# Odd heads' k by DMA, a norm with its sums from the addition, and a staged order of the work, in a four-layer attention and FFN kernel

## The chip, the cores and the metric

The kernel runs on one core of a Trainium2 chip. The metric is the device time of one execution in microseconds (us), the median of the runs shown. TensorE is called PE in the profile, VectorE DVE, ScalarE ACT, GpSimd POOL and SyncE SP. SP issues nearly all DMAs.

## The reference

Four layers follow one another on x, which has 2048 rows of 512 bf16 numbers: attention, FFN, attention, FFN, each on the normalized x and added to it, with the same weights in both pairs.

```python
def _A_ref(x, wq, wk, wv, wo, beta):        # 32 heads of 16, 4 segments of 512 rows
    q, k, v = x @ wq, x @ wk, x @ wv        # split in heads and segments
    phi = lambda t: jnp.where(t > 0, t + 1.0, jnp.exp(t))
    M = z = 0
    for s in range(4):
        p = softmax(qs @ ks.T * Dh ** -0.5 + causal_mask)      # inside the segment
        a_mem = (phi(qs) @ M) / (phi(qs) @ z + 1e-06)          # the segments before it
        outs.append(g * a_mem + (1.0 - g) * (p @ vs))          # g = sigmoid(beta), by head
        M, z = M + phi(ks).T @ vs, z + phi(ks).sum(rows)
    return concat(outs) @ wo

def _B_ref(x, w_gate, w_up, w_down):        # inner width 1792
    return gelu(x @ w_gate) * (x @ w_up) @ w_down

x = x + _A_ref(_layernorm(x), ...); x = x + _B_ref(_layernorm(x), ...)   # and both once more
```

## The kernel before

The work is cut into eight segments of 512 rows, `k` = 0 to 7: segments 0 to 3 are the first attention and FFN, 4 to 7 the second pair on the same rows. A segment is four tiles of 128 rows. x stays in `x_sb` on the chip; all weights are loaded once.

One segment's attention: a norm writes normalized rows `xn`, which are turned into `xnT` (by DMA transposes on SP, for some norms by PE transposes with `ident`); q and k come out transposed (`q`, `kf`: four blocks `b` of 128 rows, eight heads of 16 rows each), v in rows (`vaug`). A score round is four products at once on 32-row strips of PE. Even heads take their k rows straight from `kf`. For odd heads, and for rounds that take an even and an odd head together, a copy `kx` holds k with the other heads' rows at zero: 192 columns for each 128 keys, of which the first 64 hold the even heads and the other 128 the odd ones. `masked_copies` makes it with two multiplications by a column of `masks` for each block, on DVE (L417), POOL (L417) or ACT (L422). ACT takes the exponential of each pair of rounds in two instructions (L1399), POOL or DVE masks the diagonal (L1346, L1351, L1356), and a flush (L955) multiplies by v for one block and one parity of heads; DVE divides by the sums and turns the result into `aT` (L972 to L990). `wo` products follow, and DVE adds them to x (L1028). `vz` is a copy of halves of v, by DMA (L701). phi of k is turned by DMA for the memory update (L866), phi of q feeds the memory's products.

The FFN: a norm of its own (`Norm` with key `xnTf`): once a row tile is added, DVE takes statistics (L514, L522); once all four have them, POOL adds epsilon (L527) and takes the power -1/2 (L532), DVE writes four `xn` (L544). For `k` = 0, 1 and 7 (`BY_PE`) PE turns them (L586), each behind two small dummy products (`FILL`, L584). Then come 14 gate, 14 up and 4 down products of 128 rows; ACT takes gelu, for which it loads another table.

Dense products run `whole` (L476) or as four 32-column strips at once (L471, `columns`), which follows the mode of the work around them. A change of mode takes PE some time.

The order of the instructions on every engine is written out by a planner when the kernel is built. It keeps a clock for each engine, posts jobs with a time at which they are ready and a slack, and lets PE take the item with the earliest due time, score rounds when two pairs of PSUM banks are free. `POLICY` holds the due times and slacks; `CHANGES` may replace them in windows of 20 us of the planner's time, and is empty. Where PE has nothing that is ready, the planner puts a dummy product on the tile `warm`:

```python
        if bank is not None:
            if streams:
                ps = Psum()
                ps.bank = bank
                product(ps()[:, 0:P], warm[:], wide[:, 0, :])
```

SP's queue holds DMA transposes, copies of v, weight loads and outputs in one order, and an instruction that waits holds all that are behind it.

Of the kernel before, what the change touches and what calls it, by code (L numbers as in the profile page):

```python
# [18 lines left out]
P = 128  # L19
D = 512  # L20
# [11 lines left out]
VALUES = TPS * VW + 16  # L32
SCALE = DH ** -0.5
# [11 lines left out]
PAIRED = [(ki, P * ki, C, C * ki) for ki in range(TPS)]  # L45


def round_of(t):

    b, i = divmod(t, ROUNDS)  # L50
    if i == SHARED:
        return b, (0, 1), PAIRED, None
    par = int(i > SHARED)
    return b, (par,), FULL[i - par * (SHARED + 1)], DIAG[i - par * (SHARED + 1)]


BY_PE = {("xnTf", 0), ("xnTf", 1), ("xnTf", NK - 1)}
BANKS = 8
# [3 lines left out]
URGENT, SOON, NORMAL = -4.0, -1.5, 0.0  # L62
XN_BUFS = 4
BUFS = 6
FILL = 2
# [4 lines left out]
    flush_wait=60.178, piece_slack=2.474, kb_slack=40.846, mem_slack=-55.59, margin=2.052, qk_due=-2.997, e_q=-1.628,  # L70
    e_k=2.444, exp_slack=-52.211, e_slack=213.844, phi_slack=26.757, gelu_slack=17.711, act_evict=-7.207,
    first_evict=15.014, gate_step=70.271, up_due=-0.803, up_step=0.121, down_due=2.855, down_step=15.464,
    upd_due=-0.036, kb_act=30.625, vz_slack=-37.946, x_dve=-2.928, v0_due=-11.201, x1_at=-44.439, x2_at=17.127,
    x3_at=25.097, x3_load=11.502, direct=4, gelu_tiles=7, look=4.219, lag=0.576, wv_at=-5.253, xn_pool=39.635,
    kb_pool=0.131, cut_pool=-3.745, at_pool=5.073, pe_turns=0, gate_due=2.262, shun=0.829, col_gap=3.113, hold=3,
    early=122.612, starve=0.322, near=-0.26, cap=2, soon=21.81, columns=0)

CHANGES = {
}
# [12 lines left out]
class Engine:  # L92
# [24 lines left out]
    def serve(self, now):  # L117
# [9 lines left out]
        job = min((j for j in jobs if j[0] + self.LATENCY <= start + 0.03), key=lambda j: j[0] + j[1] + (  # L127
# [123 lines left out]
class Item:  # L251


    def __init__(self, due, ready, ops, done, kind, ps, after="start"):
        self.after = after
        self.due = due if callable(due) else lambda: due
        self.ready, self.ops, self.done, self.kind, self.ps = ready, ops, done, kind, ps
        self.posted = 0.0
# [27 lines left out]
def order(pol, nc, cst, seg, wrk, psp, A_x, A_wq, A_wk, A_wv, A_wo, A_beta, B_x, B_w_gate, B_w_up, B_w_down, out):  # L286
# [88 lines left out]

    tmp_e2 = cst.tile([P, H], F32, name="tmp_e2")
# [26 lines left out]

    def on_dve_or_pool(ready, slack, later, fast, slow, emit, told):

        taken = []
        ck.dve.post(ready, slack, (fast, lambda: emit(nc.vector), told), taken=taken)
        if later is not None:
            ck.pool.post(ready, slack + later, (slow, lambda: emit(nc.gpsimd), told), taken=taken)

    def masked_copies(ready, slack, kx, kf, told):
# [4 lines left out]
        def vector(which, eng):  # L416
            return lambda: eng.tensor_scalar(out=kx[:, :, C * which:C * which + P], in0=kf, scalar1=masks[:, which:which + 1],  # L417
                                             scalar2=None, op0=ALU.mult)
# [6 lines left out]
        ck.dve.post(ready, slack, (Port(0.35), vector(0, nc.vector), None),  # L425
                    (Port(0.35), vector(1, nc.vector), told), taken=taken)
        ck.pool.post(ready, slack + pol.kb_pool, (Port(1.57, True), vector(0, nc.gpsimd), None),
# [3 lines left out]
    def turn_later(t, slack, out, in_, landed, margin=0.0):  # L431
# [5 lines left out]
        ck.sp.post(t, slack, (1.3, lambda: nc.sync.dma_start_transpose(out=out(), in_=in_()), told))  # L437
# [40 lines left out]
    def soon(name, n=KT, part=1.0):  # L478

        t = ck.pe - 0.1 - ck.back  # L480
# [20 lines left out]
    class Norm:  # L501
        def __init__(self, key, tt0, tag, slack, free):
            self.key, self.tt0, self.tag, self.slack, self.free = key, tt0, tag, slack, free
            self.mv, self.n, self.left = None, 0, TPS
# [3 lines left out]

        def stats(self, j, ready):
            def emit():  # L510
                if self.mv is None:
                    self.mv = self.small("mv", 2)
# [3 lines left out]
            def told(t):  # L516
                self.n += 1
                if self.n == TPS:
                    self.scales(t)

            ck.dve.post(ready, self.slack, (0.66, emit, None),
                        (0.17, lambda: nc.vector.bn_aggr(out=self.mv[:, j, :], in_=self.st6[:]), told))  # L522

        def scales(self, ready):
            def first():
                self.ve = wrk.tile([P, TPS, 1], F32, tag="lnve", name="ve")
                nc.gpsimd.tensor_scalar(out=self.ve[:], in0=self.mv[:, :, 1:2], scalar1=EPS_LN, scalar2=None,  # L527
                                        op0=ALU.add)

            def second():  # L530
                self.rs = self.small("rs", 1)
                nc.gpsimd.tensor_tensor(out=self.rs[:], in0=self.ve[:], in1=mhalf[:], op=ALU.pow)  # L532

            ck.pool.post(ready, URGENT, (0.25, first, None),
                         (1.05, second, lambda t: ck.when(self.free, lambda: self.start(max(t, ck.pe)))))

        def start(self, ready):
            self.xnT = seg.tile([P, KT, L], BF16, tag=self.tag, bufs=1, name="xnT")
            for j in range(TPS):
                xn_slots.take(lambda n, j=j: bufs.take(lambda i: self.row(j, n, i, max(ready, ck.pe))))  # L540

        def normed(self, j, i, eng=nc.vector):
            xn = buffer(i, "xn")
            eng.tensor_scalar(out=xn[:], in0=x_sb[:, self.tt0 + j, :], scalar1=self.mv[:, j, 0:1],  # L544
# [3 lines left out]
        def row(self, j, n, i, ready):  # L548
# [13 lines left out]
            def told(t):  # L562
                if self.by_pe():
                    items.append(self.turn_item(j, xn, t, landed))
                else:
                    turn_later(t, self.slack, lambda: self.xnT[:, :, j * P:(j + 1) * P], lambda: xn()[:], landed,
# [961 lines left out]
```

## Time and profile before

| | |
|---|---|
| runs | 541.96, 542.2 and 543.59 us, median 542.2 |
| profiled execution | 543.32 us, span 541.6 |
| granted PE clock | 1.0 |
| PE busy | 522.7 us, 97% |
| DVE busy | 439.1 us, 81% |
| ACT busy | 434.3 us, 80% |
| POOL busy | 297.4 us, 55% |
| DMA q1 | 68752 packets, 26.36 MB, 24.5% of 16 engines |

The profile is of one execution. The span runs from its first to its last instruction; its own time is 1.7 us longer. Busy times are sums over the instructions. The end of a PE product is modelled, so what PE does in a stretch is read from the starts. Behind the bar of a row stands the idle time of the engine just before it, with what ended that idle time.

### The profile page before, as it was taken

The page shows a single profiled execution, that of the slowest core. Times are in us where ns is not written, and L with a number is a line of the kernel's source. Part 1 is how long each engine was busy: PE and PEld are TensorE (multiplying, and loading weights), DVE is VectorE, ACT ScalarE, POOL GpSimd, SP SyncE. Part 2 cuts the span into 40 slices and gives each one's busy share as a digit, 9 for nine tenths or more (in the row PEclk, how much of TensorE's full clock was granted, in tenths as well). Part 3 has the DMA queues.
Part 4 walks back from the last instruction along what each step waited for, and adds up shares of the span by engine and source line. Part 5 has one row for each costly group of instructions (what it writes and reads, how often), then busy time and mean ns, then how long its engine had stood idle before and what let it go on. Part 6 is the DMA issues. An engine that isn't in the chain of part 4 may idle for free.

```text
span 541.6 us, 22747 instructions
## 1 busy us (share of the span) xinstructions
PE 522.7 (97%) x10016; PEld 274.0 (51%) x10075; DVE 439.1 (81%) x814; ACT 434.3 (80%) x533; POOL 297.4 (55%) x346
## 2 busy tenths in 40 slices
PE   8899999999999999999999999999999999999997
PEld 4454555454554445554555545554465456555444
DVE  7899998899988998679987699879778786786342
ACT  5999899997998987999899899997887978910320
POOL 4887589487857986155871595716863164300000
PEclk9999999999999999999999999999999999999999
DMA  8477410620240124101332211411313014000001
GB/s 270 63 123 178 136 41 7 153 52 14 33 79 14 24 41 89 33 2 32 42 70 32 34 34 20 72 22 33 61 33 40 15 13 81 4 3 27 14 0 40
DMA packets 69141, 28.08 MB, mean 52 GB/s; under 512 B 53426, under 2 KB 69042, under 8 KB 69042
## 3 DMA queue, kind: packets, MB, share of 16 engines
q1 hardware_dynamic: 68752, 26.36, 24.5%
q8 instruction: 79, 1.29, 1.0%
q10 hardware_dynamic: 290, 0.26, 0.1%
q14 instruction: 20, 0.16, 0.1%
HBM read 9.70 MB, written 2.10 MB: 22 GB/s over the span
## 4 chain that ended last, share of the span: by engine, by line
PE 88%; DVE 6%; issue 2%; ACT 1%; DMA 1%; POOL 0%; ACTq 0%; DVEq 0%; POOLq 0%
PE ps L476 39%; PE ps L471 34%; PE ps L939 8%; PE ps L955 7%; ACT pt L1399 1%; DVE xn L544 1%; DMA xnT<-xn 1%; DVE st L514 1%; DVE x_sb L1028 1%; DMA x_sb<-in_A_x_dram 1%; PE ps L866 1%; DVE kx L417 0%; DVE st L1184 0%; DVE pt L1356 0%; DVE byq L972 0%
## 5 line engine op out<-in xcount | busy, mean ns | idle before, releaser
L1399 ACT ACTIVATE pt<-ps 128x1024 bf16<-128x1024 f32 x288 | 278.9, 1030 | 38.4 <-PE ps L939 34.1
L1346 POOL TENSOR_SCALAR_AFFINE_SELECT pt<-pt 128x256 bf16<-128x256 bf16 (+1 forms) x192 | 109.6, 584 | 132.5 <-ACT pt L1399 129.0
L1093 DVE TENSOR_TENSOR gel_sb<-gel_sb,ps 128x512 bf16<-128x512 bf16 x112 | 75.3, 683 | 33.8 <-PE ps L476 20.5
L1028 DVE TENSOR_TENSOR x_sb<-x_sb,ps 128x512 bf16<-128x512 bf16 (+1 forms) x68 | 43.1, 643 | 26.9 <-PE ps L476 16.4
L764 POOL TENSOR_SCALAR e<-e 128x512 bf16<-128x512 bf16 x39 | 61.4, 1577 | 4.6 <-ACT e L741 3.6
L476 PE MATMUL ps<-wd_sb,gel_sb 128*128 128x512 bf16 (+1 forms) x287 | 58.7, 351 | 1.5 <-issue 1.3
L972 DVE STREAM_TRANSPOSE byq<-ps 128x512 f32<-128x512 f32 x64 | 45.1, 706 | 16.1 <-PE ps L955 15.6
L471 PE MATMUL ps<-xnT,wg_sb 128*32 128x512 bf16 x916 | 56.1, 380 | 0.1
L476 PE MATMUL ps<-xnT,wu_sb 128*128 128x512 bf16 x213 | 51.1, 379 | 1.5 <-issue 1.1
L476 PE MATMUL ps<-xnT,wg_sb 128*128 128x512 bf16 x207 | 49.9, 379 | 1.6 <-issue 1.4
L471 PE MATMUL ps<-xnT,wu_sb 128*32 128x512 bf16 x888 | 51.0, 379 | 0.0
L471 PE MATMUL ps<-wd_sb,gel_sb 128*32 128x512 bf16 (+1 forms) x816 | 45.3, 361 | 0.0
L476 PEld LDWEIGHTS <-gel_sb 128*128 128x128 bf16 x300 | 27.9, 98 | 25.3 <-issue 0.4
L514 DVE BATCH_NORM_STATS2 st<-x_sb 128x6 f32<-128x512 bf16 x60 | 40.4, 673 | 0.2
L1351 POOL TENSOR_SCALAR_AFFINE_SELECT pt<-pt 64x1024 bf16<-64x1024 bf16 x26 | 32.4, 1247 | 9.8 <-ACT pt L1399 9.0
L955 PE MATMUL ps<-pt,vaug 128*32 128x256 bf16 (+2 forms) x1344 | 35.2, 238 | 1.5 <-issue 1.0
L471 PEld LDWEIGHTS <-wu_sb 128*32 128x32 bf16 x888 | 23.0, 97 | 22.3 <-issue 0.9
L955 PEld LDWEIGHTS <-vaug 128*32 128x32 bf16 x1344 | 27.6, 97 | 12.6 <-issue 4.1
L476 PEld LDWEIGHTS <-wu_sb 128*128 128x128 bf16 x226 | 20.8, 98 | 24.8 <-issue 1.2
L471 PEld LDWEIGHTS <-wg_sb 128*32 128x32 bf16 x916 | 23.4, 97 | 19.1 <-issue 1.3
L1152 ACT ACTIVATE gel_sb<-gel_sb 128x3584 bf16<-128x3584 bf16 (+1 forms) x14 | 32.4, 2351 | 0.0
L939 PE MATMUL ps<-q,kx 32*128 32x64 bf16 (+2 forms) x1120 | 31.2, 217 | 0.7 <-ACT pt L1399 0.5
(145 smaller groups left out, 892.7 us busy)
## 6 DMA issues: line engine op xcount, KB each, us to landing
vz<-vaug SPq DMA_DIRECT2D x14, 136.0 KB, 3.0
wg_sb<-in_B_w_gate_dram SPq DMA_DIRECT2D x8, 224.0 KB, 3.6
wu_sb<-in_B_w_up_dram SPq DMA_DIRECT2D x8, 224.0 KB, 2.9
wd_sb<-in_B_w_down_dram SPq DMA_DIRECT2D x7, 256.0 KB, 4.4
x_sb<-in_A_x_dram SPq DMA_DIRECT2D x3, 512.0 KB, 6.5
out_dram<-x_sb SPq DMA_DIRECT2D x12, 128.0 KB, 1.7
xnT<-xn SPq DMA_TRANSPOSE x48, 2.9
wk_sb<-in_A_wk_dram SPq DMA_DIRECT2D x2, 256.0 KB, 4.7
```

The lines of the kernel that those rows point to most:

```text
L471: nc.tensor.matmul(out[r], lhsT=lhsT[:, r], rhs=rhs, start=start, stop=stop, tile_position=(0, 32 * c))
L476: nc.tensor.matmul(out, lhsT=lhsT, rhs=rhs, start=start, stop=stop)
L514: nc.vector.bn_stats(out=self.st6[:, 0, :], in_=x_sb[:, self.tt0 + j, :])
L764: lambda eng: eng.tensor_scalar(out=e[0][:], in0=e[0][:], scalar1=1.0, scalar2=None, op0=ALU.min), summed)
L939: nc.tensor.matmul(ps_all[:, bank, o + c0:o + c0 + n], lhsT=lhsT, rhs=self.q[rows, b, q0:q0 + n], start=True, stop=True, tile_position=(32 ...
L955: nc.tensor.matmul(ps()[32 * j:32 * j + 32, q0:q0 + n], lhsT=va[:, ki * VW + g:ki * VW + g + 32], rhs=pt_all[:, places[i], j, c0:c0 + n], ...
L972: nc.vector.transpose(out=self.byq[:, par, :, :].rearrange("p a c -> p (a c)"), in_=ps()[:])
L1028: ck.dve.post(ck.made(), slack, (0.15 + 0.00104 * (c1 - c0), lambda: nc.vector.tensor_tensor(out=xt, in0=xt, in1=ps()[:, 0:c1 - c0], op=AL ...
L1093: ck.dve.post(ck.made(), NORMAL, (0.683, lambda: nc.vector.tensor_tensor(out=g, in0=g, in1=ps()[:], op=ALU.mult), lambda t: (ps.read(t), e ...
L1152: return (0.205 + 0.427 * (f1 - f0), lambda: nc.scalar.activation(out=g, in_=g, func=ACT.Gelu_apprx_tanh), lambda t: self.gelu_done(t, f0, ...
L1346: nc.gpsimd.affine_select(out=view, in_=view, pattern=[[0, 4], [0, n], [1, C]], compare_op=ALU.is_ge, fill=0.0, base=C, channel_multiplier=-1)
L1399: nc.scalar.activation(out=pt_all[:, s0:s0 + 2, 2 * p:2 * p + 2, :].rearrange("p r h c -> p h r c"), in_=ps_all[:, pair[0]:pair[1] + 1, :] ...
```

## The change

Five things change.

1. For segments 1 to 3 (`SENT`) the odd heads' columns of `kx` come from `kf` by four DMAs for a segment, 16 partitions each, once all four blocks of `kf` are there. The engines write the 64 columns of the even heads alone, one instruction for a block. Both `kx` tiles have those columns zeroed once by DVE: one ahead of the first statistics, the other by a job at 14 us of the planner's time. Segments 0 and 4 to 7 keep both masked copies; the first now writes 64 columns of each 128.
2. The norm of FFN 1 (`QUICK`): for row tiles 0, 1 and 2 the addition of `wo` also gives the sum of each row, DVE makes two multiples of the mean of it, and ACT sums the squares of the difference. Row tile 3 keeps DVE's statistics. POOL's two steps and `xn` go by pairs of row tiles.
3. `FILL` is 0: no small dummies ahead of the PE transposes.
4. `POLICY` has new values, and three sets of `STAGES` replace them from 80, 160 and 260 us of the planner's time. Weights must have landed by the planner's clock before a gate or down product is taken. Costs of some jobs are set anew (DMA transposes 1.34 for 1.3, loads 0.59 for 0.57). Gate products of FFN 0 may start ahead of the memory update, in another order of the 14.
5. Rounds and flushes come from tables, which could also take segments in halves; `HALVED` is empty, so rounds and flushes of a segment stand as before.

Of the products on PE, all but dummies are the same in number and width; `whole` and `columns` are shared out anew. By the two lists, before and after: full dummies behind the twelve at the start 44 and 30, small ones 24 and 0; changes of tile mode 300 and 299; loads of an ACT table 14 and 14.

The core of the diff:

```diff
+HALVED = ()
+SENT = (1, 2, 3)
...
 BY_PE = {("xnTf", 0), ("xnTf", 1), ("xnTf", NK - 1)}
+QUICK = {("xnTf", 1): (0, 1, 2)}
...
-FILL = 2
+FILL = 0
...
-CHANGES = {
-}
+STAGES = [
+    (4, 8, dict(
...
+    (8, 13, dict(
...
+    (13, 60, dict(
...
+CHANGES = {w: change for w0, w1, change in STAGES for w in range(w0, w1)}
...
+    nc.vector.memset(means[:, 0:1], -float(D) ** -1.5)
+    nc.vector.memset(means[:, 1:2], 1.0 / D)
+    nc.vector.memset(kxs[1][:, :, :, C:3 * C], 0.0)
...
+    ck.dve.post(14.0, pol.zero_slack, (Port(0.95), lambda: nc.vector.memset(kxs[0][:, :, :, C:3 * C], 0.0),
+                                       lambda t: ev.update({("zero", 2): t})))
...
-    def masked_copies(ready, slack, kx, kf, told):
+    def masked_copies(ready, slack, kx, kf, even, told):
...
+        if even:
+            ck.dve.post(ready, slack, (Port(0.28), vector(0, nc.vector), told), taken=taken)
+            ck.pool.post(ready, slack + pol.kb_pool, (Port(0.93, True), vector(0, nc.gpsimd), told), taken=taken)
+            ck.act.post(ready, slack + pol.kb_act, (0.51, scalar(0), told), taken=taken)
+            return
...
+            def add():
+                self.moments()
+                made.append(wrk.tile([P, 1], F32, tag="rowsum", bufs=4, name="rowsum"))
+                nc.vector.scalar_tensor_tensor(out=xt, in0=ps()[:], scalar=1.0, in1=xt, op0=ALU.mult, op1=ALU.add,
+                                               accum_out=made[0][:])
+
+            def mean():
+                nc.vector.tensor_tensor(out=self.mv[:, j, 0:2], in0=made[0][:].to_broadcast([P, 2]), in1=means[:], op=ALU.mult)
+
+            def square():
+                nc.scalar.activation(out=junk[:], in_=xt, func=ACT.Square, scale=float(D) ** -0.5, bias=self.mv[:, j, 0:1],
+                                     accum_out=self.mv[:, j, 2:3])
+
+            ck.dve.post(ck.made(), slack, (0.76, add, ps.read), (0.15, mean, lambda t: ck.act.post(
+                t, slack, (0.95, square, self.told(j)), table="exp")))
...
+                for r in list(parts):
+                    ck.sp.post(ck.pe, pol.kd_slack, (0.64, lambda r=r: nc.sync.dma_start(
+                        out=kx[r:r + 16, :, C:3 * C], in_=kf[r:r + 16, :, :]), told))
...
-                    add_to_x(j, ps, URGENT, lambda t: self.norm.stats(j, t))
+                    if j in self.norm.quick:
+                        self.norm.added(j, ps, self.norm.urge(j))
+                    else:
+                        add_to_x(j, ps, self.norm.urge(j), lambda t: self.norm.stats(j, t))
...
-                            lambda: ck.has(("xnTf", k)) and (("down", k - 1) if k else ("upd", 0)) in ev,
+                            lambda: ck.has(("xnTf", k), ("loaded", "first")) and (k == 0 and ft >= HELD or (("down", k - 1) if k else ("upd", 0)) in ev),
```

More of the change, by code (lines that the diff above doesn't have):

```diff
@@ L32 @@
 VALUES = TPS * VW + 16
+HELD = -(-VALUES // L)
 SCALE = DH ** -0.5
@@ L528, in first @@
                                         op0=ALU.add)
             def second():
[L531 to L539, printed above, removed]
+                if self.rs is None:
+                    self.rs = self.small("rs", 1)
@@ new lines, in second, with start @@
+                nc.gpsimd.tensor_tensor(out=self.rs[:, j0:j0 + n, :], in0=self.ve[:], in1=mhalf[:, 0:n, :], op=ALU.pow)
+            ck.pool.post(ready, min(self.urge(j0), URGENT), (0.25, first, None),
+                         (1.05, second, lambda t: ck.when(self.free, lambda: self.start(max(t, ck.pe), j0, n))))
+        def start(self, ready, j0, n):
+            if self.xnT is None:
+                self.xnT = seg.tile([P, KT, L], BF16, tag=self.tag, bufs=1, name="xnT")
+            for j in range(j0, j0 + n):
```

331 lines of the change are left out of this document (226 added, 105 removed).

## The prediction

> **What bounds the kernel now.** I read the page's busy shares first, then TensorE's instructions in order of time, then the other engines' rows for the places where TensorE stands still.
>
> ```profile
> PE 522.7 (97%) x10016; PEld 274.0 (51%) x10075; DVE 439.1 (81%) x814; ACT 434.3 (80%) x533; POOL 297.4 (55%) x346
> L471 PE MATMUL ps<-warm 128*32 128x128 bf16 x88 | 2.9, 222 | 0.4 <-ACT pt L1399 0.3 <-ACT wd_sb L462 0.2
> L476 PE MATMUL ps<-warm 128*128 128x128 bf16 x22 | 2.6, 219 | 0.3 <-ACT pt L1399 0.3
> L584 PE MATMUL ps<-warm 128*128 128x32 bf16 x24 | 2.5, 178 | 0.1
> 510.65 1.89 PE L476 MATMUL ps<-xnT,wu_sb 128*128 128x512 bf16 x8
> 512.38 1.89 PE L476 MATMUL ps<-xnT,wg_sb 128*128 128x512 bf16 x8
> ```
>
> TensorE is busy all the time, with the same useful products in both kernels, so the time can only move through its idle places. Eight full products start 1.73 us apart (510.65 to 512.38): 0.216 us each. The three `warm` groups are dummies that the order puts where it has nothing to run: 88/4 + 22 = 44 full ones and 24 small ones. 12 full ones lie before 26 us, and 25 of the others in two stretches, which begin behind the last output projection (`wo`) of segments 0 and 1 and end at the first gate product of their FFNs.
>
> ```profile
> 69.07 1.89 PE L476 MATMUL ps<-wv_sb,xnT 128*128 128x512 bf16 x8
> 70.89 0.29 PE L939 MATMUL ps<-q,kx 32*128 32x64 bf16 x8
> 71.22 0.63 PE L955 MATMUL ps<-pt,vaug 128*32 128x256 bf16 x24
> 71.79 0.51 PE L471 MATMUL ps<-warm 128*32 128x128 bf16 x24
> 75.40 0.40 PE L586 MATMUL ps<-ident,xn 128*128 128x128 bf16 x4
> 75.69 0.38 PE L586 MATMUL ps<-ident,xn 128*128 128x128 bf16 x4
> 78.80 1.55 PE L471 MATMUL ps<-xnT,wg_sb 128*32 128x512 bf16 x24
> ```
>
> ```profile
> 129.36 1.04 PE L471 MATMUL ps<-wd_sb,gel_sb 128*32 128x512 bf16 x16
> 137.47 0.40 PE L586 MATMUL ps<-ident,xn 128*128 128x128 bf16 x4 [0.70 <-DVE xn L544]
> 138.55 1.05 PE L471 MATMUL ps<-xnT,wg_sb 128*32 128x512 bf16 x16
> ```
>
> The columns are start, duration (its end is modelled, so I use differences of starts), instruction, count, idle time before it. Stretch 1 lasts from 69.07 to 78.80, 9.7 us. Useful in it: 8 value products 1.8 (69.07 to 70.89); four score pairs at 0.33 (70.89 to 71.22) 1.3; two flushes at 0.57 (71.22 to 71.79) 1.1; four turns of xn, at most 0.29 each, 1.0; the memory update, some 0.4 (an estimate: 64 instructions of 32 columns, where the flush's 40 wider ones take 0.57). That is 5.6, so **4.1 us are dummies and waits**. Stretch 2 lasts from 129.36 to 138.55, 9.2 us: 14 down products 3.0, four score pairs 1.3, a flush 0.6, the turns 1.0, together 5.9, so **3.3 us are lost**. The releaser in it is the normalized row, DVE L544: the FFN's norm is what TensorE waits for.
>
> **The change, part by part.** I compare the two instruction lists, engine by engine; they hold no times.
>
> *Stretch 1.* The norm of FFN 0 is not rewritten; its steps stand in the same order on DVE, POOL and ScalarE.
>
> ```profile
> 69.32 1.26 DVE L1028 TENSOR_TENSOR x_sb<-x_sb,ps 128x512 bf16<-128x512 bf16 x2
> 73.91 1.85 DVE L544 TENSOR_SCALAR xn<-x_sb,mv,rs 128x512 bf16<-128x512 bf16 x4
> 77.94 0.41 DVE L461 COPY xnT<-ps 128x512 bf16<-128x512 bf16 x1
> ```
>
> From the first addition at 69.32 over xn to the last copy at 77.94 its 9.7 us stay. But behind the last `wo` group the new order has 20 products of q, k and v where the old one has 8: 12 more at 0.216 fill 2.6 us, less two changes of tile mode (0.1 each, an estimate: a score pair with the change behind it takes 0.33, and its 512 columns would take 0.22): **-2.4 us**. That holds if their old place, the first 60 us, does not become idle for want of them. There ScalarE sets the pace:
>
> ```profile
> 10.50:60.00 49.50, 47.10 (x872) 23.62 (x880) 46.23 (x99) 47.83 (x65) 38.60 (x42) 1.00 0.63 138
> L422 ACT ACTIVATE kx<-kf,masks 128x512 bf16<-128x512 bf16 x3 | 2.2, 721 | 0.0
> L422 ACT ACTIVATE kx<-kf,masks 128x256 bf16<-128x256 bf16 x3 | 1.5, 515 | 0.3 <-DVE kf L461 0.3
> ```
>
> In the first row the fourth busy time is ScalarE's: 47.83 of 49.5 us. Its three pairs of masked copies (2.2 + 1.5) become two half copies (2 x 0.515), because the DMAs carry the odd heads: 2.7 us less, as much as the 12 products that leave. The exponentials of segment 0 end as much earlier. So the cover is paid for by the DMAs. Bounds: -3.2 (all but 0.9 covered) to -1.0 (most of it reopens earlier).
>
> *The twelve DMAs.* Four per segment on SP's queue. Nearest rows: a pair of value copies, 64 partitions each, issue and landing.
>
> ```profile
> 119.82 1.32 SPq L701 DMA_DIRECT2D vz<-vaug  x2
> vz<-vaug SPq DMA_DIRECT2D x14, 136.0 KB, 3.0
> 60.02 1.05 SPq L305 DMA_DIRECT2D wu_sb<-in_B_w_up_dram  x2
> 33.00:53.00 20.00, 19.47 (x366) 9.37 (x365) 18.48 (x34) 19.10 (x27) 16.10 (x19) 1.00 0.78 177
> ```
>
> At 0.66 each, four cost SP 2.6 us and land 3 us later. Segment 1's first score pair that reads them stands 21 us of products (at 0.216 per 512 columns) behind the last k product, so 5.6 us are hidden. Eight of them stand ahead of the last FFN weights: these are issued till 61.1, would now be till 66.4, land 3 us later, and the gate products begin at some 76. Hidden too, with 7 us to spare. Taken at 0; from below there is nothing beyond ScalarE's 2.7; from above, see the rivals.
>
> *Stretch 2.* Rows 0 to 2 of FFN 1's norm get their sum from the addition and their squares from ScalarE, in two pairs of rows.
>
> ```profile
> 129.32 1.25 DVE L1028 TENSOR_TENSOR x_sb<-x_sb,ps 128x512 bf16<-128x512 bf16 x2
> 132.11 0.66 DVE L514 BATCH_NORM_STATS2 st<-x_sb 128x6 f32<-128x512 bf16 x1
> 133.45 0.23 POOL L527 TENSOR_SCALAR ve<-mv 128x4 f32<-128x4 f32 x1
> 134.84 2.57 DVE L544 TENSOR_SCALAR xn<-x_sb,mv,rs 128x512 bf16<-128x512 bf16 x4
> L522 DVE BATCH_NORM_AGGREGATE mv<-st 128x2 f32<-128x6 f32 x60 | 10.9, 182 | 2.1
> L745 DVE SCALAR_TENSOR_TENSOR e<-kf,e 128x512 bf16<-128x512 bf16 x20 | 16.4, 822 | 0.0
> L1200 ACT ACTIVATE pt<-x_sb,shift 128x512 bf16<-128x512 bf16 x1 | 0.7, 722 | 0.0
> L1194 POOL TENSOR_TENSOR rs<-mv,mhalf 128x2 f32<-128x2 f32 x2 | 1.5, 752 | 2.8 <-DVE mv L1190 2.8
> ```
>
> Before: 4.1 us from the last `wo` group to the last statistics (another segment's among them), then POOL, then xn till 137.4. After, from the end of the last `wo` group: its addition 0.8; statistics and aggregate of row 3, 0.9, so 1.7; POOL's two steps on two rows, 0.23 + 0.75 with gaps, 3.0. By the list a down addition stands next on DVE; its 14 products end at some 3.4 (3.0 plus a score pair), so 4.1; xn 2, a copy, xn 3, some 1.4, so 5.5; turn and copy, 0.9: the gate begins at **6.4 instead of 9.2**, with 5.9 us of useful work on TensorE beside it. Rows 0 and 1 are turned before. An addition that also sums I take from L745, 0.82, a square from L1200, 0.72, and its read, for which 0.2 is my guess between DVE's 0.08 at the like place and the square itself: neither is last, row 3 is. That gives -2.8; POOL has two slow steps queued ahead of the first pair and ScalarE's exponentials queue behind the three squares, so I take **-2.0**, from -2.9 to -0.5.
>
> *The rest.* The listed dummies go from 44 full ones to 30: 16 to 7 in stretch 1, 9 to 5 in stretch 2 (7.4 us lost over 25 is 0.3 each, which gives -2.7 and -1.2, near the sums above), 7 to 4 ahead of FFN 0's down products and 2 new ones in its up products: **-0.3**. All 24 small ones go; the 8 before the last FFN stand in no wait, at some 0.03 to 0.06 each: **-0.3**.
>
> ```profile
> 26.95 1.05 PE L471 MATMUL ps<-wv_sb,xnT 128*32 128x512 bf16 x16 [0.82 <-DMA xnT<-xn]
> 2.48 0.15 DVE L374 TENSOR_REDUCE masks<-bd 128x1 f32<-128x4 f32 x1
> 3.72 1.29 DVE L1184 BATCH_NORM_STATS2 st<-x_sb 128x6 f32<-128x512 bf16 x2 [1.09 <-DMA x_sb<-in_A_x_dram]
> L342 DVE MEMSET vz<- 128x1096 uint32 x1 | 1.0, 972 | 0.2 <-issue 0.2
> ```
>
> At 26.95 a flush now stands ahead of the value products that wait 0.82 for a transposed row: **-0.3**, between -0.8 and 0. At the start the zeroing of one tile (some 0.9 by L342) and two tiny ones fall between 2.63 and the first statistics at 3.72: they end at about 3.8, **+0.1** (0 to 0.3). The second zeroing takes a place on DVE from which 1.6 us of masked copies went: 0. The profiled execution took 543.3 for a span of 541.6. **Sum: -2.4 - 2.0 - 0.3 - 0.3 - 0.3 + 0.1 = -5.2**, so 538.1 for a profiled execution; this one lies 1.1 above the median of 542.2, so **537.0** for the median.
>
> **The rivals.**
>
> *The cover reopens earlier (chance 0.15).* If ScalarE's evictions, of which the new list has two more among the first 36 exponentials (1.2 us), eat the freed 2.7, the 12 products leave a hole before 60 us. Then stretch 1 brings 1 us or none, and the sum is -2 to -4: 538.2 to 540.2. For it: ScalarE at 97% there. Against it: the list has the same 12 dummies as before up to 26 us, and none from there to stretch 1.
>
> *SP's queue blocks (0.10, slower).* The DMAs wait for all four k tiles of their segment and everything behind them on SP waits too: transposed rows of segment 3, weights of FFN 0. They go while the DMA engines are 78% busy (33 to 53 us). Each us beyond the 7 to spare holds the gate, and all after it, by a us; from 12 us of blocking the gain is gone, and 15 give 545. Against it: the value copies land in 3.0 us beside the same loads.
>
> *TensorE's clock falls, and nothing is gained (0.04).* The dummies may be what keeps the clock up.
>
> ```profile
> L349 PE MATMUL ps<-warm 128*128 128x512 bf16 x12 | 4.8, 584 | 1.1 <-DVE warm L340 1.1
> 120.00:140.00 20.00, 18.35 (x481) 10.53 (x477) 19.57 (x40) 16.87 (x22) 16.18 (x21) 1.00 0.08 17
> ```
>
> The twelve at the start take 4.8 us, 0.40 each: TensorE begins at half speed, though the granted clock (third number from the right of the second row) reads 1.00 in the stretch with the longest waits. If it fell to half in both stretches for as long as those twelve take, that is 2.4 us lost in each: 537.0 + 4.8 = 541.8. Against it: useful products stand where the dummies stood, and no wait that I find is as long as the 0.70 at 137.47. [...]
>
> **How the numbers follow.** The forecast has 0.71, with a range of its own from 534.5 to 539.5 (the terms' ends, not all at once). All gains at their best ends (-3.2, -2.9, -0.9 if the two new dummies cost nothing, -0.5, -0.8) are -8.3, 533.8, and a bit below it is less than the scatter of the runs before; the first rival reaches 540.2, and 541 takes in its tail. So 533.5 to 541.0 leaves out 0.10 + 0.04 and a little of the tails. 0.3% (1.6 us) is about what a measurement of this kernel can tell from no change: faster 0.85, same 0.05, slower 0.10.
>
> **What would show it.** In the profile after: the first gate of FFN 1 some 6.5 us behind its last `wo` product, that of FFN 0 still 9 to 10 us behind but with few dummies between; ScalarE's 36th exponential 2 to 3 us earlier; the copies of odd k landing within some 4 us and no TensorE wait on them; no new wait above 0.5 us after 140 us. Wrong it would be if the idle time ahead of the two gates is as long as before, or if SP's weight loads end after 73 us.

## The result: 536.7 us for 542.4, and the profile after

The changed kernel takes 536.72 us (median of four runs, 536.29 to 536.94), the kernel before 542.38 beside it (541.96 to 543.59): ratio 0.9892, 95% interval 0.9879 to 0.9905. The prediction was 537.0, faster. The profiled execution took 536.73 us for a span of 534.8; that of before 543.32 for 541.6.

The page after, its row of engines, and some of TensorE's instructions in order of time through stretch 1 (start, duration, count, idle time before it):

```profile
PE 526.8 (99%) x9803; PEld 270.1 (51%) x9803; DVE 432.7 (81%) x814; ACT 433.8 (81%) x544; POOL 280.2 (52%) x344
65.19 1.04 PE L559 MATMUL ps<-wo_sb,aT 128*128 128x512 bf16 x4
66.06 1.03 PE L559 MATMUL ps<-xnT,wk_sb 128*128 128x512 bf16 x4
71.83 0.28 PE L559 MATMUL ps<-warm 128*128 128x128 bf16 x2
73.33 1.01 PE L712 MATMUL ps<-ident,xn 128*128 128x128 bf16 x15
74.91 0.66 PE L1015 MATMUL ps<-gel_sb,phik 128*32 128x32 bf16 x64 [0.57 <-ACT pt L1589]
76.81 1.91 PE L554 MATMUL ps<-xnT,wg_sb 128*32 128x512 bf16 x32 [0.16 <-ACT xnT L545]
```

The last `wo` group ends at 66.06 (before at 69.07), the first gate of FFN 0 stands at 76.81 (before 78.80): it comes 2.0 us earlier, though the stretch between them has grown from 9.7 to 10.75 us. TensorE is at 99% now, where it was at 97%. Not all of that is gain: the profile of before has 10075 weight loads for 10016 products, that of after 9803 for 9803, so some 59 products of before left no record, and the gaps look idle. Stretch 2, with the last copy of a turned row:

```profile
126.10 1.68 PE L554 MATMUL ps<-wd_sb,gel_sb 128*32 128x512 bf16 x28
129.57 0.61 PE L712 MATMUL ps<-ident,xn 128*128 128x128 bf16 x8
132.09 0.42 DVE L544 COPY xnT<-ps 128x512 bf16<-128x512 bf16 x1
132.67 0.29 PE L1086 MATMUL ps<-q,kf 16*128 16x64 bf16 x6 [0.38 <-ACT pt L1589]
133.01 1.25 PE L559 MATMUL ps<-xnT,wg_sb 128*128 128x512 bf16 x5
```

From the end of the last `wo` group to the first gate of FFN 1 it is 126.10 to 133.01, 6.9 us (before 9.2). The first turn of a normalized row stands without a wait, 3.5 us behind the last `wo`. The last copy of the norm ends at 132.51, 6.4 us behind the last `wo`; the gate follows 0.5 later, behind a score round that waits 0.38 for an exponential. The gate is now 5.5 us earlier than before (138.55). Of the 6.8 us between the two spans, 1.3 are left for the rest, and the profiled execution of before had two single waits there that end on nothing the profile shows:

```profile
378.48 0.26 PE L955 MATMUL ps<-pt,vaug 128*32 128x192 bf16 x3 [1.05 <-issue]
406.61 0.29 PE L939 MATMUL ps<-q,kf 16*128 16x64 bf16 x6 [0.41 <-issue]
```

1.05 + 0.41 is as much as what is left. In the kernel before without its dummies (below) the same two places wait 0.51 and 0.47, so a part of them belongs to the order and a part to that execution. By the medians the kernels differ by 5.7 us, so behind the first gate of FFN 1 the change brought about little, some 0.2. The largest waits of TensorE after 10 us, in the view of waits (total, times, longest):

```profile
PE ps L559 <- DVE byq L1134: 0.7, 1, 0.7
PE ps L1086 <- ACT pt L1589: 0.7, 2, 0.4
PE ps L1015 <- ACT pt L1589: 0.6, 1, 0.6
```

No DMA is among them.

### The profile page after: what moved, and what is told of

Its sections match the earlier page's. It is cut to its first block, busy times and chain, and to the rows that moved or that the text cites. A ratio compares the mean times of both kernels' runs of the same rounds, so it can differ in the third digit from the quotient of the medians.

```text
span 534.8 us, 22313 instructions
## 1 busy us (share of the span) xinstructions
PE 526.8 (99%) x9803; PEld 270.1 (51%) x9803; DVE 432.7 (81%) x814; ACT 433.8 (81%) x544; POOL 280.2 (52%) x344
## 4 chain that ended last, share of the span: by engine, by line
PE 89%; DVE 5%; ACT 4%; issue 1%; POOL 1%; ACTq 0%; DVEq 0%; POOLq 0%
PE ps L559 43%; PE ps L554 30%; PE ps L1086 8%; PE ps L1115 6%; ACT pt L1589 2%; DVE st L620 1%; DVE gel_sb L1277 0%; ACT wd_sb L545 0%; PE ps L1015 0%; DVE x_sb L1206 0%; DVE byq L1134 0%; DVE e L894 0%; DVE st L1368 0%; DVE xn L670 0%; PE ps L712 0%
## 5 line engine op out<-in xcount | busy, mean ns | idle before, releaser
L559 PE MATMUL ps<-xnT,wg_sb 128*128 128x512 bf16 x279 | 65.5, 380 | 0.0
L559 PE MATMUL ps<-xnT,wu_sb 128*128 128x512 bf16 x269 | 62.0, 379 | 0.0
L554 PE MATMUL ps<-wd_sb,gel_sb 128*32 128x512 bf16 (+1 forms) x860 | 49.9, 368 | 0.2 <-issue 0.2
L554 PE MATMUL ps<-xnT,wg_sb 128*32 128x512 bf16 x676 | 41.5, 380 | 0.2 <-ACT xnT L545 0.2
L554 PE MATMUL ps<-xnT,wu_sb 128*32 128x512 bf16 x716 | 41.1, 379 | 0.1
L559 PEld LDWEIGHTS <-wg_sb 128*128 128x128 bf16 x279 | 25.7, 98 | 29.7 <-issue 0.9
L559 PEld LDWEIGHTS <-wu_sb 128*128 128x128 bf16 x269 | 25.2, 98 | 29.8 <-issue 0.7
L544 DVE CAST gel_sb<-ps 128x512 bf16<-128x512 f32 x42 | 28.4, 681 | 6.7 <-PE ps L559 4.0
L1115 PEld LDWEIGHTS <-vaug 128*32 128x32 bf16 x1344 | 27.8, 97 | 10.5 <-issue 1.6
L1336 ACT ACTIVATE gel_sb<-gel_sb 128x2048 bf16<-128x2048 bf16 (+3 forms) x22 | 32.3, 1540 | 0.0
L1086 PEld LDWEIGHTS <-kx 32*128 32x128 bf16 x1120 | 16.6, 92 | 29.0 <-issue 28.4
```

The costliest lines, as they stand in the source:

```text
L554: nc.tensor.matmul(out[r], lhsT=lhsT[:, r], rhs=rhs, start=start, stop=stop, tile_position=(0, 32 * c))
L559: nc.tensor.matmul(out, lhsT=lhsT, rhs=rhs, start=start, stop=stop)
L1086: nc.tensor.matmul(ps_all[:, bank, o + c0:o + c0 + n], lhsT=lhsT, rhs=self.q[rows, b, q0:q0 + n], start=True, stop=True, tile_position=(32 ...
L1115: nc.tensor.matmul(ps()[32 * j:32 * j + 32, q0:q0 + nq], lhsT=va[:, ki * VW + g:ki * VW + g + 32], rhs=pt_all[:, places[t], j, o:o + nq], ...
```

## The experiments

Ten of the twelve kernels keep the order of all instructions that they share with the kernel they start from; one moves some of DVE's and ScalarE's, and one is planned anew. Differences are from ratios to the kernel before, measured beside it, and 0.9892 for the changed kernel. A ratio's interval is 0.0012 to 0.0024 to either side, 0.7 to 1.3 us.

| kernel | us | ratio, 95% interval |
|---|---|---|
| `stats_by_dve` | 538.03 | 0.9914, 0.9899 to 0.9929 |
| `norm_in_one` | 537.59 | 0.9909, 0.9895 to 0.9922 |
| `norm_old_same_order` | 540.86 | 0.9968, 0.9955 to 0.998 |
| `act_copies` | 537.38 | 0.9902, 0.9889 to 0.9916 |
| `kx_copies_same_order` | 541.75 | 0.9985, 0.9973 to 0.9997 |
| `kx_odd_on_dve` | 538.48 | 0.993, 0.9918 to 0.9942 |
| `dma_x3` | 545.1 | 1.0046, 1.0034 to 1.0058 |
| `dma_x6` | 558.3 | 1.0302, 1.0278 to 1.0326 |
| `after_no_dummies` | 536.3 | 0.9887, 0.9874 to 0.99 |
| `before_no_dummies` | 544.38 | 1.0041, 1.0025 to 1.0056 |
| `kx_by_engines` | 545.36 | 1.0052, 1.0039 to 1.0065 |
| `turns_first_no_dummies` | 538.63 | 0.9922, 0.9908 to 0.9935 |

**FFN 1's norm, taken back in halves and whole.** `stats_by_dve`:

```diff
-                nc.vector.scalar_tensor_tensor(out=xt, in0=ps()[:], scalar=1.0, in1=xt, op0=ALU.mult, op1=ALU.add,
-                                               accum_out=made[0][:])
+                nc.vector.tensor_tensor(out=xt, in0=xt, in1=ps()[:], op=ALU.add)
...
-                nc.vector.tensor_tensor(out=self.mv[:, j, 0:2], in0=made[0][:].to_broadcast([P, 2]), in1=means[:], op=ALU.mult)
+                nc.vector.bn_stats(out=st6[:, 0, :], in_=xt)
+                nc.vector.bn_aggr(out=self.mv[:, j, 1:3], in_=st6[:])
...
-                nc.scalar.activation(out=junk[:], in_=xt, func=ACT.Square, ...)
```

> The changed kernel (536.7 us) with the order of every engine kept, but rows 0 to 2 of FFN 1's norm take their statistics from DVE again (0.69 + 0.18 us each, in place of a 0.16 us multiple and a sum that rides on the addition), and ScalarE makes no squares. Pairs of rows stay. Theory (the norm's chain is what TensorE waits for, and moving statistics off DVE shortens it): DVE gets 3 x 0.7 = 2.1 us more ahead of row 3's statistics, at a place where it stands nearly without a pause, so the first gate of FFN 1 comes 1.3 to 2.1 us later and the time is 538.0 to 538.8. Rival (the gain is in the new order alone, the kind of instruction is indifferent): within 0.4 of 536.7.

`norm_in_one`: POOL's steps once, issued ahead of the first xn.

```diff
-                nc.gpsimd.tensor_tensor(out=self.rs[:, j0:j0 + n, :], in0=self.ve[:], in1=mhalf[:, 0:n, :], op=ALU.pow)
+            nc.gpsimd.tensor_tensor(out=self.rs[:], in0=ve[:], in1=mhalf[:], op=ALU.pow)
```

> The changed kernel with the order kept, squares on ScalarE kept, but POOL's two steps of FFN 1's norm made once for all four rows, behind row 3's statistics (so xn of rows 0 and 1 waits for row 3). Theory: the first xn starts at 129.4 instead of 127.9 us of the profile (aggregate done at 128.0, then 0.23 + 1.04 with gaps), and the gate follows 0.8 to 1.6 later: 537.5 to 538.3. Rival (row 3 sets the gate in any case, the pairs only bring rows 0 and 1 forward into time that is free): within 0.4 of 536.7.

`norm_old_same_order` has both edits.

> Both of the two together: FFN 1's norm as before the change, in the order of the changed kernel. Theory: the 2.0 us that the prediction gave to this norm come back, and somewhat more, since the new order has no cover for the wait: 538.7 to 540.2. Rival (the order makes the gain): within 0.5 of 536.7.

Measured: 1.2, 0.9 and 4.1 us slower than the changed kernel. The interval of each of the first two overlaps that of the changed kernel, so the place in the trace has to carry them. TensorE's first turned row behind the down products, in the kernel with DVE's statistics, then in the one with POOL's steps made once, then in the one with the whole old norm:

```profile
130.64 0.72 PE L712 MATMUL ps<-ident,xn 128*128 128x128 bf16 x8 [0.81 <-DVE xn L670]
130.50 0.72 PE L727 MATMUL ps<-ident,xn 128*128 128x128 bf16 x8 [0.24 <-DVE xn L685]
132.58 1.06 PE L727 MATMUL ps<-ident,xn 128*128 128x128 bf16 x8 [2.65 <-DVE xn L685]
```

In the changed kernel there was no wait, and from the last `wo` to the gate it was 6.9 us. In the three kernels it is 8.9 (126.20 to 135.13, the end of it at half clock, see the last section), 7.7 (126.53 to 134.21) and 10.8 (126.30 to 137.08). The theory holds: the norm's chain is what TensorE waits for, and both halves of its rewriting shorten it. Together they are worth twice the sum of their single prices. Most of the surplus is the clock, which fell in all five executions of the whole old norm (mean granted clock 0.996 or 0.997). In the table by stretches of the whole old norm (span of the stretch, busy time of PE, PEld, DVE, ACT, POOL, granted clock, DMA):

```profile
129.40:132.40 3.00, 0.54 (x3) 0.04 (x1) 1.49 (x3) 0.95 (x2) 1.93 (x4) 1.00 0.00 0
133.00:136.00 3.00, 3.00 (x63) 2.08 (x62) 2.57 (x6) 2.18 (x3) 0.00 (x0) 0.50 0.00 0
```

Behind the long wait TensorE runs at half the granted clock until about 136.2: a flush in it takes 1.19 us (134.88 to 136.07), the same flush 0.67 in the changed kernel (130.92 to 131.59). If the work of those 3.4 us takes half of them at full clock, an estimate from the granted 0.50, up to 1.7 us are lost; 2.65 + 1.7 is 4.35, against 4.1 by the ratio. In the kernel before, the same norm cost no clock (granted 1.00 from 120 to 140): dummies and other products stood in its wait, and without the dummies the clock falls behind it there too (at 140.1, last section).

**ScalarE's work.** `act_copies` adds four copies ahead of exponentials of segment 0.

```diff
+EXTRA = [(0, t) for t in (12, 16, 20, 24)]
...
             def exp(p=p, pair=pair):
+                if pair is pairs[0] and rounds[0] in EXTRA:
+                    nc.scalar.activation(out=junk[:].rearrange("p (a b) -> p a b", a=4), in_=wide, func=ACT.Copy)
```

> The changed kernel with the order kept and four more copies of 128x512 on ScalarE (0.65 to 0.7 us each, 2.7 in sum, about what the masked copies cost it before) ahead of four exponentials of segment 0, between 25 and 45 us. Theory (ScalarE sets the pace up to 60 us, so the 2.7 us freed there are what lets 12 products move behind the last wo): 2.0 to 2.7 us slower, 538.7 to 539.4. Rival (ScalarE has slack there, its 97% busy is queueing): within 0.5 of 536.7.

Measured: 0.5 slower; the theory falls. The first of the extra copies and the exponential behind it, then the 35th and 36th exponentials with the copies and without, and the first gate of FFN 0 with them:

```profile
26.19 0.76 ACT L1591 ACTIVATE junk<-warm 128x512 bf16<-128x512 bf16 x1
26.71 3.90 ACT L1592 ACTIVATE pt<-ps 128x1024 bf16<-128x1024 f32 x4
55.02 1.94 ACT L1592 ACTIVATE pt<-ps 128x1024 bf16<-128x1024 f32 x2 [0.16 <-PE ps L1087]
54.48 1.94 ACT L1589 ACTIVATE pt<-ps 128x1024 bf16<-128x1024 f32 x2 [0.16 <-PE ps L1086]
77.35 1.91 PE L555 MATMUL ps<-xnT,wg_sb 128*32 128x512 bf16 x32 [0.16 <-ACT xnT L546]
```

The next exponential starts 0.52 behind the start of a copy of 0.76 (each row holds time that the next instruction overlaps), so four copies take 2.1 us of the engine, and both the exponentials and the gate came 0.54 later. ScalarE had some 1.5 us to give in a stretch where it is busy 97% of the time (48.13 of 49.5 us from 10.5 to 60 in the changed kernel). So the 2.7 us of masked copies that it lost paid for a small part of the 12 products at most.

**Who makes the odd copies.** `kx_copies_same_order` lets the engine that copies the even heads copy the odd ones too, with no DMA; `kx_odd_on_dve` gives the odd ones to DVE.

```diff
-            ck.pool.post(ready, slack + pol.kb_pool, (Port(0.93, True), vector(0, nc.gpsimd), told), taken=taken)
+            ck.pool.post(ready, slack + pol.kb_pool, (Port(0.93, True), two(vector, nc.gpsimd), told), taken=taken)
...
-                    ck.sp.post(ck.pe, pol.kd_slack, (0.64, lambda r=r: nc.sync.dma_start(
-                        out=kx[r:r + 16, :, C:3 * C], in_=kf[r:r + 16, :, :]), told))
+                    ck.sp.post(ck.pe, pol.kd_slack, (0.64, lambda: None, told))
```

> The changed kernel with the order kept, but without the twelve kx DMAs: odd heads' columns are copied by the engine that copies the even ones, right behind (per copy 0.72 us on ScalarE, 1.6 on POOL, 0.35 on DVE; in the first 110 us two, four and two of them carry segments 1 and 2). Theory (the DMAs take work off engines that set the pace before 60 us): ScalarE gets 1.4 us back, POOL 6: 1.0 to 2.5 us slower, 537.7 to 539.2. Rival (the copies lie in free time of the engines, the DMAs bring nothing): within 0.4 of 536.7.

> As the kernel without the twelve kx DMAs and in the kept order, but each odd copy on DVE (0.35 us, 12 of them, 2.8 us of DVE in the first 110 us), wherever the even one is made. Theory (the 5 us that the engines' copies cost came through GpSimd, whose longer copies stood ahead of diagonal masks): 0.3 to 1.5 us slower than the changed kernel, 537.0 to 538.2, and no wait on a mask. Rival (any engine that carries the copies is late by as much, DVE being the chain of the norms): 3 us slower or more, 540.

Measured: 5.0 and 2.1 slower than the changed kernel. The first ran at two clocks: in six of its twelve executions the mean granted clock was 1.0 (540.8 to 541.6 us), in the other six 0.997 (541.9 to 542.9). The six at full clock are 4.4 slower than the changed kernel. GpSimd's queue in the first of them, and the flush that waits for its last mask:

```profile
50.39 2.46 POOL L495 TENSOR_SCALAR kx<-kf,masks 128x256 bf16<-128x256 bf16 x2
52.81 2.12 POOL L1540 TENSOR_SCALAR_AFFINE_SELECT pt<-pt 128x512 bf16<-128x512 bf16 x4
53.52 0.30 PE L1117 MATMUL ps<-pt,gel_sb 128*32 128x64 bf16 x8 [2.67 <-POOL pt L1540]
```

An even and an odd copy take GpSimd 2.46 us and stand ahead of the diagonal masks; the flush waits 2.67. With the odd copies on DVE that wait is gone; 2.1 us stay, a little over the range expected. One new wait of 0.69 for DVE shows (119.57, the memory update), the rest is in no single place. So of the 5.0 us that the DMAs bring in this order, some 2.3 come through GpSimd, 2.1 stay where DVE makes the copies, and the rest is clock.

`kx_by_engines` is the one planned anew, with `SENT = ()`:

> The changed kernel with SENT empty: all odd copies on the engines, and the order planned anew for it (66 full dummies for 30). Theory (in a free order the copies go back to DVE mostly, and only the cover of stretch 1 is lost): 1.5 to 3 us slower than the changed kernel, 538.2 to 539.7. Rival (the planner makes up for it): within 0.5 of 536.7. Rival (the engines cannot carry them at all beside the new norm): 541 or more.

Measured: 8.7 slower than the changed kernel, 2.8 slower than the one before; the third expectation held in its number. But an order planned with due times that were set for another kernel is no measure of the copies alone: this one has 66 full dummies where the kernel before, which makes the same copies, has 44. It says only that these due times need the DMAs.

**SP's queue.** `dma_x3` and `dma_x6` issue two and five more DMAs behind each of the twelve.

```diff
+                        nc.sync.dma_start(out=kx[r:r + 16, :, C:3 * C], in_=kf[r:r + 16, :, :])
+                        for n in range(2):
...
+                            nc.sync.dma_start(out=rows, in_=kf[r:r + 16, :, :])
```

> The changed kernel with the order kept; each of the twelve kx DMAs is followed on SP's queue by two more of the same size (64 KB, from kf to rows of the output that are written over at the end). SP has 5.3 us more in each of segments 1 to 3. Theory (SP has time to spare, as the trace after shows: last FFN-0 weight load issued at 62.5, first up product at 93.2 us): within 0.5 of 536.7. Rival (SP's queue is nearly on the path, as the prediction had it with 7 us to spare for two segments): 10.6 us later weights, 3 us slower or more, 540.

> The same with five more behind each: SP has 13 us more in each of the three segments. Theory: now the transposed rows and phi of k that stand behind them on SP come 13 to 26 us late, and TensorE waits for them: 2 to 15 us slower. Rival (even that is hidden): within 0.5 of 536.7. By the prediction's count (7 us to spare, 26 us added): 19 us slower.

Measured: 8.4 and 22.2 slower. With two more, the theory fell and the rival held in its size, at another place. In the changed kernel two copies of v stand on SP behind eight of the DMAs. Their issue, the last weights, the landing time of the copies, the flush that reads them and the first up product; below, the flush and the stretch behind it with two more:

```profile
59.80 1.39 SPq L850 DMA_DIRECT2D vz<-vaug  x2
61.23 1.27 SPq L373 DMA_DIRECT2D wu_sb<-in_B_w_up_dram  x2
DMA to landing us min/median/max: 6.8/7.0/7.3
68.45 0.29 PE L1115 MATMUL ps<-pt,vz 128*32 128x64 bf16 x16
93.22 2.32 PE L559 MATMUL ps<-xnT,wu_sb 128*128 128x512 bf16 x10
```

```profile
75.77 0.41 PE L1121 MATMUL ps<-pt,vz 128*32 128x64 bf16 x16 [5.39 <-DMA vz<-vaug]
76.00:81.00 5.00, 4.83 (x64) 1.72 (x54) 1.79 (x4) 2.00 (x3) 0.00 (x0) 0.59 0.62 100
```

The flush at 68.45 needs the first of the two copies: in `dma_x3` it waits for the one that is issued first, at 70.5, and starts when that has landed, 5.2 later. In the changed kernel the first copy is issued at 59.80 and lands 7.3 later: 67.1 for a flush at 68.45. There is some 1.3 us to spare, not 7. The weights did have room: the last up load is issued by 62.5, the first up product stands at 93.2. With two more the flush waits 5.39 (q's products before it 1.5 for a transposed row), and the granted clock reads 0.59 from 76 to 81. With five more the flushes wait 13 us for the copies of v, and q's products 6.8 for a transposed row. Those 22.2 lie above the theory's 15; the 19 of the prediction's count is nearer, but it counted the weights, at another place.

**The dummies.** `after_no_dummies` and `before_no_dummies` leave the dummies out; both keep the twelve at the start.

```diff
-                product(ps()[:, 0:P], warm[:], wide[:, 0, :])
...
-            ops = [(Clocks.MM[512] / 2, whole(lambda: nc.tensor.matmul(
-                ps()[:, half:half + 32], lhsT=warm[:], rhs=wide[:, 0, 0:32], start=True, stop=True)))] * fill
+            ops = [(Clocks.MM[512] / 2, whole(lambda: None))] * fill
```

> The changed kernel with the order kept and its 30 full dummies behind the twelve at the start left out (they compute nothing that is used). Theory (a dummy marks idle time and costs nothing itself; the clock holds): within 0.4 of 536.7, granted clock 1.0. Rival (dummies hold up what becomes ready beside them, 0.1 each): 534 to 536. Rival (they keep the clock up): 1 us slower or more, a granted clock below 1.

> The kernel before with the order kept, its 44 full and 24 small dummies left out. Theory (the small ones cost 0.03 to 0.06 each in the turns of the norms, the full ones about 0.01 as in the changed kernel): 0.3 to 1.2 us faster than the kernel before, 541.2 to 542.1. Rival (they keep the clock up): slower, a granted clock below 1. By the side: the profile shows whether the two single waits of 1.2 and 0.6 us behind 377 and 406 us in the profile of before belong to the order or to that execution.

Measured: in the changed kernel 0.3 faster, inside the scatter; in the kernel before 2.2 us slower, the rival. The tables by stretches, first the kernel before without dummies (two rows), then before as it was, then the changed kernel without dummies:

```profile
71.50:74.50 3.00, 1.44 (x60) 0.92 (x52) 2.96 (x8) 3.00 (x4) 2.58 (x5) 1.00 0.12 24
75.50:82.00 6.50, 6.12 (x121) 3.03 (x122) 5.71 (x10) 5.67 (x9) 6.09 (x6) 0.50 0.16 43
```

```profile
75.50:82.00 6.50, 6.12 (x186) 4.45 (x189) 6.12 (x11) 6.50 (x11) 6.08 (x6) 1.00 0.16 45
```

```profile
73.50:77.00 3.50, 2.10 (x95) 1.85 (x97) 3.22 (x8) 3.50 (x6) 2.18 (x3) 1.00 0.03 5
```

In the order before, the dummies kept the clock: without them TensorE is busy for 1.44 of 3 us in stretch 1, and then runs at half speed for some 7 us. All six executions without them show a lowered mean clock, from 0.997 in three (543.6 to 544.0 us) to 0.990 (the profiled one, 545.6), so the 2.2 us are the middle of some 1 to 4. In the new order useful products stand there and the clock stays (1.0 or 0.999 in all four executions). Why it stays is not shown by the busy share: in the stretch above TensorE is busy 2.10 of 3.5 us, 60%, and in other kernels the clock fell behind such a share (last section).

**A further step on stretch 1.** `turns_first_no_dummies` makes DVE copy all four turned rows (`copy` is DVE's in both posts) before it goes on; what stands between is held until then.

```diff
+            ck.dve.post(ck.made(), slack, (0.673, copy, end), taken=taken)
+            ck.act.post(ck.made(), slack + pol.act_evict, (0.602, copy, end), taken=taken)
...
+            if self.key == ("xnTf", 0):
+                self.made = getattr(self, "made", 0) + 1
+                if self.made == TPS:
+                    HOLD["on"] = TPS
```

> The kernel without dummies (536.3 us), order kept but for DVE and ScalarE in FFN 0's norm: all four copies of turned rows (xnT) are made by DVE right behind the four xn, ahead of a flush's turn, reciprocal and scaling (1.9 us), where two of the four stood on ScalarE behind two exponentials. Theory (the copies of turned rows, not the normalized rows, are what the first gate of FFN 0 now waits for: the last two start on ScalarE at 75.58 and the gate at 76.81): the gate 0.7 to 1.3 us earlier, 535.0 to 535.6. Rival (the gate then waits as long for the flush's bank or the scores): within 0.3 of 536.3.

In it the held turn of the flush reads its bank after the bank has gone to a later product, so one flush's values are replaced by another product's; the time is read for the order. Measured: 1.9 slower than the kernel without dummies. Most of that is clock: the two executions with a mean granted clock of 1.0 took 536.8 and 537.2 us, the four with 0.997 took 538.6 to 539.0. In the profiled execution, one of the four, DVE's copies, and TensorE's way to the gate:

```profile
73.79 1.42 DVE L547 COPY xnT<-ps 128x512 bf16<-128x512 bf16 x4 [0.59 <-PE ps L740]
77.32 0.40 PE L1115 MATMUL ps<-q,kx 32*128 32x256 bf16 x12 [1.73 <-DVE macc L1072]
77.65 2.69 PE L578 MATMUL ps<-xnT,wg_sb 128*32 128x512 bf16 x24
77.00:81.00 4.00, 3.68 (x48) 1.54 (x51) 2.55 (x7) 2.46 (x3) 2.60 (x4) 0.60 0.00 0
```

The copies are done at 75.2 instead of 76.8, but the round of scores ahead of the gate waits 1.73 for a bank that DVE's copy of the memory (macc) frees behind the held work, the gate comes at 77.65 (76.82 without this step), and the granted clock reads 0.60 from 77 to 81. The rival held in its place, a wait for a bank, though not in its size: in both orders tried, what DVE does first chooses who waits. That DVE bounds stretch 1 in any order is not shown. None of the kernels beats the changed one by more than the scatter.

## Why the prediction was right

*Stretch 2, -2.0.* Right: 9.2 us became 6.9, -2.3, between the -2.8 of the steps and the -2.0 taken. POOL's two steps go by pairs, and the last copy ends 6.4 behind the last `wo`, as worked out; the 0.5 to the gate is a score round that waits for an exponential, and that the working did not have.

*Stretch 1, -2.4.* Mis-sized: the 12 products moved, but the chain did not keep its 9.7 us. Useful in its 10.75 us are 20 products 4.3, and as before scores 1.3, flushes 1.1, turns 1.0, memory 0.5 (74.91 to the next start at 75.40): 8.2. So 2.5 are lost where 4.0 were by the same count, -1.5. The step that failed is "its 9.7 us stay". The moved products bring their evictions along, and one stands ahead of xn on DVE:

```profile
70.01 1.04 POOL L657 TENSOR_TENSOR rs<-ve,mhalf 128x4 f32<-128x4 f32 x1
71.16 0.69 DVE L544 CAST vaug<-ps 128x512 bf16<-128x512 f32 x1 [0.35 <-PE ps L559]
71.77 1.43 DVE L670 TENSOR_SCALAR xn<-x_sb,mv,rs 128x512 bf16<-128x512 bf16 x4
```

The scale is ready at 71.05, DVE waits 0.35 for a value product and evicts it, and xn starts at 71.77, 5.7 us behind the last `wo`; before it was 4.8. This is read from the trace: no run takes that eviction away or moves the 12 products back, so the -1.5 is a count and not a measured difference.

*Who pays for it.* Wrong in its reason. The 35th and 36th exponentials in the profile of before:

```profile
57.40 1.94 ACT L1399 ACTIVATE pt<-ps 128x1024 bf16<-128x1024 f32 x2
```

The 36th ends 2.9 us earlier now (54.48 + 1.94 for 57.40 + 1.94), within the 2 to 3 that I gave, and I read ScalarE's 97% as the bound. Four extra copies cost 0.54; it was GpSimd and DVE that could not carry the copies in this order.

*The twelve DMAs at 0.* Right as a price:

```profile
kx<-kf SPq DMA_DIRECT2D x12, 64.0 KB, 2.6
```

They land in 2.6 us, no product waits on them, the last weights are issued by 62.5. Wrong in the spare: "7 us to spare" was worked out for the weights, but the copies of v stand on the same queue with 1.3, and land 7 us behind their issue where 3 were taken. The rival named the right queue, and its threshold was far off.

*The clock, 0.04.* Right for this change, and the reason against it, that useful products stand where the dummies stood, held. The dummies of the kernel before were worth 2.2 us, so an order with fewer dummies and no new cover could have paid a price near the one that I put on this rival (2.4 for a stretch). The other one, that no wait is as long as the 0.70 at 137.47, was read from a trace in which the dummies stood around that wait: with them the granted clock reads 1.00 from 120 to 140, without them it fell to half at 140.1.

*The small terms.* The wait of 0.82 at 26.95 went, but one of 0.68 for a flush's turn came at 28.54, so -0.3 was about 0. The start memset cost nothing: the first statistics begin at 3.63 for 3.72. Small dummies and other places (-0.6): the change brought 1.3 us more between the first gate of FFN 0 and the last `wo` of segment 1 (2.0 earlier became 3.3). A score pair that moved behind that point accounts for 0.2 of it and two dummies fewer for 0.4; the rest stays open.

By the landmarks: 2.0 us by the gate of FFN 0, 5.5 by that of FFN 1, with -4.9 forecast for both stretches and the small terms ahead of them. The medians say 5.7, the forecast 5.2. That the sum came so near is in part luck: stretch 1 brought 0.9 less than its term, and the 1.3 just named, of which the working had 0.3, made up for it. The lower end of the gains, 533.8, is 533.9 by its own terms (542.2 - 8.3); nothing hangs on it.

## What to carry to other kernels

Before a dummy, a wait or a busy share is given a price, change that one thing with the order kept: an engine at 97% had 1.5 us to give, and a queue that looked free had 1.3. For each queue that an added instruction is put on, the spare is that of the tightest instruction behind it, not of the most bytes. Here useful work in the place of dummies brought the idle time and the clock stayed; the dummies were worth their clock only as long as nothing better stood there (2.2 us in the kernel before, none in the changed one), and work that is moved into a gap brings its evictions with it.

## What the runs showed that was not expected

The granted clock went to half behind stretches that were far from empty. In the kernel before without dummies it fell behind 3 us in which TensorE was busy for 1.44, and in `stats_by_dve` behind 1.81 of 3 us:

```profile
129.60:132.60 3.00, 1.81 (x28) 1.01 (x26) 2.96 (x8) 1.80 (x3) 2.11 (x4) 1.00 0.00 0
133.00:136.00 3.00, 2.78 (x69) 2.03 (x59) 2.36 (x6) 1.69 (x3) 0.46 (x1) 0.50 0.02 5
```

It did not fall in `kx_copies_same_order`, behind 0.36 of 3 us:

```profile
50.50:53.50 3.00, 0.36 (x16) 0.16 (x12) 0.51 (x1) 1.94 (x3) 3.00 (x4) 1.00 0.92 261
53.50:60.00 6.50, 6.42 (x146) 3.42 (x150) 5.26 (x9) 4.82 (x6) 2.31 (x5) 1.00 0.82 283
```

How long half clock lasts is read from the half microseconds in which it begins and ends, with the old norm and in the kernel before without dummies:

```profile
132.50:133.00 0.50, 0.42 (x4) 0.23 (x4) 0.50 (x3) 0.00 (x0) 0.34 (x1) 0.76 0.00 0
136.00:136.50 0.50, 0.50 (x19) 0.42 (x7) 0.00 (x0) 0.35 (x1) 0.08 (x1) 0.83 0.00 0
```

```profile
75.00:75.50 0.50, 0.50 (x10) 0.50 (x9) 0.50 (x3) 0.50 (x3) 0.42 (x1) 0.75 0.07 4
82.00:82.50 0.50, 0.50 (x16) 0.10 (x4) 0.00 (x0) 0.41 (x1) 0.50 (x1) 0.92 0.00 0
```

0.76 means half clock from 132.76 on, 0.83 until 136.17: 3.4 us. By the other two rows 75.25 to 82.08, twice that. In the latter trace the clock falls once more, behind stretch 2:

```profile
140.00:140.50 0.50, 0.47 (x11) 0.23 (x8) 0.47 (x2) 0.50 (x3) 0.43 (x2) 0.60 0.00 0
143.50:144.00 0.50, 0.50 (x15) 0.23 (x8) 0.50 (x2) 0.00 (x0) 0.50 (x1) 0.98 0.00 0
```

That is 140.1 to 143.5, again 3.4 us, and it begins 64.85 us behind the first fall, 19 times 3.413. So in this execution the two lengths at half clock, 6.83 and 3.4, and the 64.85 from fall to fall are all multiples of some 3.41 us, the length with the old norm. What sets that length no run here shows.

The same kernel can fall or not. By the mean granted clock, 0.997 for 1.0, `kx_copies_same_order` did in six of twelve executions, `turns_first_no_dummies` in four of six, and `stats_by_dve` in one of four (the profiled one, 539.24 us at 0.997; the others 537.76 to 538.06 at 1.0). The instructions and their order are the same in these, so something that changes from one execution to the next decides; what it is, no run here shows. The busy share alone does not decide: the clock fell behind 1.44 of 3 us (48%) and 1.81 of 3 us (60%), and it held behind 0.36 of 3 us (12%) and, in `after_no_dummies`, through 2.10 of 3.5 us (60%). Whether the kind of work counts stays open.
